# One kernel, two orders: the first transfers split over two queues, and another table of planned times

## The chip, the core and the metric

The kernel runs on one core of a Trainium2 chip. The metric is device time in microseconds (us) for one execution; less is better. The core has engines that run side by side, each through its own list of instructions in the order in which they were written: TensorE (PE, matrix products and transposes; its weight loads are shown as PEld), VectorE (DVE), ScalarE (ACT), GpSimd (POOL) and SyncE (SP, which here only starts transfers). Engines wait for one another through semaphores. Transfers (DMA) are started by an instruction on SP or ACT and then run by themselves on 16 shared DMA engines.

## The reference

Two layers, each a gated convolution (A) and a feed-forward network (B), with a residual around each. S is 2048 rows, D is 512, F is 1792; everything is bf16.

```
def A(q, k, v, shift_k, ssm_k, ssm_D):
    k_shift = sum over t in 0..3 of shift(k, t) * shift_k[:, t]   # short causal filter per channel
    kv = k_shift * v
    y  = causal convolution of kv with ssm_k along S               # 2048 taps, by FFT
    return q * (y + kv * ssm_D)

def B(x, w_gate, w_up, w_down):
    return (silu(x @ w_gate) * (x @ w_up)) @ w_down

x = A_q
for layer in (0, 1):
    x = x + A(layernorm(x), A_k, A_v, A_shift_k, A_ssm_k, A_ssm_D)
    x = x + B(layernorm(x), B_w_gate, B_w_up, B_w_down)
```

The factor that the layer norm feeds (`q` in A) is only multiplied in at the end, so the convolution of kv with ssm_k is the same in both layers and is computed once.

## The kernel before

**Blocks.** The 2048 rows are cut into four blocks c = 0..3 of 512 rows, and each block into two halves h of 256 rows. A triple (layer, c, h) names a unit of the feed-forward network, so there are 16 units. The convolution works by blocks: a block of ssm_k (`hn`, transposed to `hs`) and a block of kv become spectra `H` and `X` by matrix products with a table of cosines and sines (`fwd`), spectra are multiplied (`product`) into `Z`, and a product with the transposed table (`inv`) gives `Y`.

**Opening.** Nothing but this is on the way to the first feed-forward unit: load the first ssm_k block (`load_h`, line 412), the first k block (`load_k`, line 417) and the four filter taps per channel (`load_taps`, line 1033); transpose each on PE (lines 540, 431 and 1086); build diagonal matrices `dg` from the taps (lines 1091, 1093, 1097); apply the short filter on PE (`shift_mul`, line 560, shown as line 387, the helper `mm`) and multiply by v on DVE (line 575); spectra, products, inverse; then `n` and `xc` (lines 886 to 891), the statistics (line 796), `rstd` on POOL (line 801), `z` (line 851), its transposes on PE (`ptz`, line 903), copied to `zT` on ACT and DVE (lines 908, 906). Then unit (0,0,0) starts.

**Feed-forward unit.** `ffn`: 14 column blocks of F in groups of 4, 4, 4 and 2. PE writes gate and up products into PSUM (`pf`, four buffers), ACT takes them out as `sg` (line 949) and `ht` (line 953), DVE multiplies them (line 956), PE multiplies with `wd_sb` into `pd` (line 969). While these run, the other engines do the convolution and the layer norms of later blocks (`conv`, `prologue`).

**What sets the order.** The kernel records every step as an `Op` with an engine and an assumed cost, and `Plan.forward` lays out each engine's list: among the steps that can go next it takes the one with the earliest possible start, and among equals the one with the smallest due time. The due times are the table `DUE`, one entry for each op in the order of recording (`plan.dues(DUE)`, line 1188). The chip then runs each engine's list as it stands. Assumed delays from the issue of a transfer to its landing are constants such as `LH0` (first ssm_k block) and `LK0` (first k block). They shape the order and nothing else.

**Fillers.** Where the layout leaves PE idle for over 0.5 us in its first 32 us, `issue` puts in matrix products of the identity with itself whose result nobody reads (`wm`, line 1193); there are 24 at the start and 6 later. They wait for `ident`, which POOL makes (masks.py, lines 197 and 199).

**Choices by unit.** Small tables say which engine does a step for a given (layer, c, h): `ST1` and `ST2` put the statistics of a layer norm on ACT in place of DVE, `N_ACT` and `Z_ACT` put the normalising step on ACT, and `X_PE` adds the residual on PE with a product by the identity (line 928) in place of DVE. For (0,0,0) and (0,0,1) the first prologue has its own path, so the entries of `ST2`, `Z_ACT` and `N_ACT` for these two are not read; the last unit (1,3,1) adds its residual on PE whether or not `X_PE` has it.

**The first issues.** `HQ` chooses the order:

```
    if HQ == "ACT":
        tr = load_taps()
        k0 = load_k(0, -69.8, after=[tr])
    elif HQ == "k":
        ...
    else:
        h0 = load_h(0, "SP", -70)
        k0 = load_k(0, -69.9, after=[h0])
        tr = load_taps([k0])
```

With `HQ == "ACT"` the load `h0` has already been put on ACT's own queue (line 1029). After these, SP issues the row for ssm_D (`drow`, line 1046), the first v block (`vt`), the first x block (`xc`), the second ssm_k and v blocks, the gate weights, and two transposing transfers of the table (`inv`, line 1104).

Of the kernel before, what the change touches and what calls it, by code (L numbers as in the profile page):

```python
# [13 lines left out]
ACT = mybir.ActivationFunctionType  # L14
# [7 lines left out]
ST2 = lambda l, c, h: (l, c, h) in {(0, 0, 0), (0, 2, 1), (1, 2, 1)}  # L22
# [4 lines left out]
Z_ACT = lambda l, c, h: (l, c, h) in {(0, 0, 1), (0, 2, 0), (1, 0, 0), (1, 1, 0), (1, 1, 1)}  # L27
N_ACT = lambda l, c, h: (l, c, h) in {(0, 0, 1), (0, 2, 1), (0, 3, 0), (1, 0, 0), (1, 1, 1), (1, 3, 1)}
GROUPS = (4, 4, 4, 2)
TINY = 0.2  # L30
LH0 = 3.3
LK0 = 4.2
HQ = 'h'
# [4 lines left out]
X_PE = lambda l, c, h: (l, c, h) in {(0, 0, 0), (0, 2, 1), (1, 1, 0), (1, 3, 1)}  # L38
RINGS = {}
DUE = [2, 0, 0, 6, 3, 7, 5, 0, 6, 12, 18, 24, 32, 10, 12, 14, 8, 18, 24, 26, 28, 22, 24, 31, 37, 35, 44, 40, 46, 53, 38, 58, 41, 46, 43, 49, 46, 51,  # L40
       64, 80, 69, 96, 76, 88, 80, 90, 50, 56, 57, 71, 78, 85, 66, 65, 72, 68, 60, 62, 70, 1, 54, 59, 56, 77, 58, 74, 61, 84, 104, 60, 148, 204, 211,
       217, 84, 87, 91, 94, 102, 96, 99, 101, 108, 114, 73, 113, 115, 118, 126, 89, 103, 106, 111, 120, 104, 112, 119, 121, 131, 139, 143, 170, 193,
       176, 200, 132, 108, 122, 135, 145, 126, 139, 150, 130, 141, 143, 155, 148, 160, 153, 165, 173, 179, 158, 162, 172, 166, 175, 183, 171, 179,
       188, 184, 188, 195, 192, 196, 207, 201, 205, 212, 153, 159, 169, 166, 185, 191, 212, 203, 197, 206, 231, 215, 219, 225, 234, 238, 209, 217,
       214, 226, 229, 235, 231, 240, 233, 250, 238, 245, 250, 255, 261, 269, 293, 298, 295, 303, 241, 253, 252, 254, 309, 325, 263, 265, 311, 313,
       247, 259, 256, 258, 267, 269, 327, 329, 315, 317, 274, 338, 323, 265, 265, 272, 283, 287, 277, 298, 292, 299, 301, 304, 314, 320, 327, 317,
       322, 328, 332, 343, 350, 352, 369, 391, 395, 412, 414, 424, 417, 433, 440, 448, 462, 454, 461, 464, 467, 483, 486, 496, 493, 508, 345, 334,
       375, 369, 363, 356, 382, 393, 271, 284, 302, 297, 313, 324, 240, 260, 305, 283, 308, 320, 391, 398, 474, 481, 452, 464, 388, 402, 441, 450,
       419, 431, 421, 436, 471, 477, 500, 489, 526, 561, 543, 578, 224, 326, 331, 353, 404, 422, 511, 532, 549, 567, 585, 603, 645, 663, 680, 691,
       706, 719, 761, 750, 787, 854, 793, 781, 821, 829, 869, 883, 882, 893, 817, 824, 843, 872, 887, 905, 930, 942, 281, 307, 336, 364, 345, 360,  # L50
       353, 381, 362, 376, 416, 463, 443, 371, 386, 380, 393, 393, 407, 402, 440, 465, 493, 502, 410, 445, 423, 455, 432, 460, 454, 469, 477, 519,
       511, 476, 500, 484, 505, 523, 528, 532, 535, 541, 537, 558, 545, 577, 554, 572, 563, 582, 597, 616, 651, 572, 586, 581, 614, 589, 609, 598,
       624, 656, 668, 694, 607, 619, 624, 636, 633, 645, 642, 654, 674, 685, 703, 659, 679, 677, 688, 703, 711, 716, 719, 724, 731, 548, 550, 562,
       570, 574, 591, 593, 595, 602, 614, 621, 628, 640, 634, 642, 644, 647, 662, 665, 674, 672, 687, 738, 773, 744, 774, 781, 783, 799, 803, 807,
       814, 826, 838, 832, 840, 842, 845, 860, 865, 863, 878, 720, 732, 729, 741, 738, 749, 746, 758, 775, 825, 834, 755, 767, 764, 776, 773, 785,
       782, 793, 820, 873, 895, 790, 802, 799, 811, 808, 820, 843, 859, 866, 886, 904, 851, 871, 860, 876, 884, 916, 912, 924, 919, 991, 1028, 999,
       834, 843, 849, 852, 864, 881, 885, 899, 902, 916, 924, 954, 978, 960, 978, 981, 983, 997, 1003, 1000, 1016, 966, 988, 972, 981, 990, 995,
       1012, 1015, 1019, 1027, 1034, 1048, 1040, 1047, 1055, 1058, 1115, 1120, 1118, 1133, 887, 909, 898, 904, 942, 930, 955, 917, 1050, 1058, 1028,
       1036, 973, 986, 1017, 1025, 995, 1003, 1039, 1047, 976, 981, 1006, 1014, 1065, 1076, 1094, 1088, 1100, 1106, 1122, 1144, 1069, 1102, 1108,
       1075, 1089, 1115, 1095, 1082, 1165, 1183, 1177, 1200, 1122, 1206, 1128, 1149, 1133, 1209, 1221, 1250, 1237, 1262, 1275, 1302, 1340, 1325,  # L60
       1330, 1344, 1357, 1322, 1335, 1347, 1352, 1388, 1396, 1366, 1374, 1390, 1401, 1368, 1379, 1408, 1419, 1431, 1438, 1444, 1450, 1316, 967, 1215,
       1395, 1156, 1167, 1184, 1197, 1239, 1262, 1277, 1289, 1462, 1473, 1488, 1500, 1512, 1523, 1540, 1568, 1586, 1635, 1659, 1647, 1677, 1683,
       1680, 1688, 1702, 1716, 1659, 1670, 1693, 1701, 1665, 1692, 1710, 1729, 1747, 1777, 1804, 1815, 1834, 1864, 1852, 1878, 1896, 1913, 921, 933,
       930, 941, 938, 950, 947, 959, 982, 1061, 1070, 956, 968, 965, 976, 978, 991, 987, 998, 1006, 1087, 1078, 997, 1009, 1008, 1020, 1019, 1031,
       1030, 1042, 1049, 1096, 1104, 1041, 1053, 1052, 1064, 1112, 1222, 1192, 1237, 1213, 1250, 1291, 1287, 1113, 1140, 1122, 1135, 1130, 1144,
       1139, 1156, 1178, 1227, 1253, 1148, 1161, 1157, 1172, 1166, 1223, 1174, 1190, 1233, 1270, 1262, 1183, 1195, 1196, 1232, 1205, 1218, 1214,
       1227, 1256, 1279, 1288, 1235, 1247, 1244, 1256, 1273, 1301, 1296, 1308, 1304, 1316, 1305, 1317, 1314, 1325, 1327, 1340, 1336, 1347, 1355,
       1428, 1462, 1349, 1362, 1357, 1369, 1371, 1384, 1379, 1391, 1399, 1454, 1471, 1392, 1406, 1401, 1413, 1410, 1422, 1419, 1431, 1456, 1480,
       1488, 1436, 1454, 1445, 1459, 1484, 1501, 1497, 1509, 1504, 1534, 1323, 1337, 1329, 1336, 1339, 1342, 1364, 1361, 1368, 1376, 1383, 1395,
       1389, 1396, 1398, 1401, 1437, 1440, 1449, 1447, 1462, 1552, 1564, 1558, 1565, 1567, 1570, 1585, 1588, 1595, 1605, 1612, 1619, 1631, 1625,  # L70
       1632, 1634, 1637, 1653, 1656, 1666, 1663, 1678, 1532, 1534, 1506, 1517, 1514, 1526, 1523, 1535, 1536, 1548, 1579, 1624, 1606, 1545, 1557,
       1554, 1566, 1563, 1574, 1571, 1583, 1597, 1650, 1672, 1580, 1607, 1589, 1602, 1598, 1612, 1615, 1642, 1653, 1663, 1685, 1633, 1680, 1641,
       1675, 1689, 1706, 1698, 1742, 1705, 1749, 1713, 1617, 1625, 1632, 1635, 1646, 1654, 1659, 1703, 1707, 1723, 1741, 1758, 1770, 1764, 1800,
       1803, 1806, 1826, 1830, 1840, 1842, 1852, 1771, 1802, 1788, 1801, 1827, 1830, 1845, 1849, 1856, 1890, 1907, 1918, 1929, 1950, 1953, 1964,
       1976, 1981, 2006, 2011, 2009, 2024, 1726, 1710, 1721, 1747, 1780, 1792, 1767, 1755, 1857, 1873, 1905, 1913, 1888, 1893, 1890, 1898, 1859,
       1868, 1803, 1809, 1792, 1800, 1790, 1795, 1924, 1936, 1947, 1953, 1959, 1965, 1988, 1977, 2057, 1978, 2039, 1985, 2084, 2064, 2070, 2006,
       2097, 2077, 2022, 2090, 2051, 2108, 2134, 2146, 2097, 2119, 2156, 2169, 2181, 2206, 2194, 2240, 2259, 2267, 2275, 2265, 2270, 2331, 2338,
       2311, 2317, 2289, 2295, 2287, 2300, 2333, 2343, 2309, 2321, 2351, 2363, 2374, 2380, 2386, 2392, 2090, 2012, 2024, 2041, 2063, 2074, 2085,
       2108, 2216, 2404, 2415, 2433, 2451, 2465, 2477, 2489, 2502, 2526, 2514, 2538, 2556, 2550, 2544, 2553, 2561, 2566, 2574, 2628, 2635, 2615,
       2622, 1711, 1732, 1719, 1737, 1728, 1752, 1737, 1757, 1794, 1831, 1870, 1746, 1762, 1755, 1767, 1763, 1775, 1772, 1784, 1828, 1840, 1879,  # L80
       1781, 1804, 1794, 1814, 1805, 1819, 1814, 1825, 1846, 1862, 1969, 1822, 1837, 1849, 1863, 1875, 1901, 2039, 1908, 2046, 2053, 2065, 2061,
       1892, 1904, 1907, 1924, 1916, 1935, 1925, 1940, 1971, 2030, 2060, 1933, 1945, 1942, 1960, 1951, 1972, 1960, 1992, 2000, 2043, 2069, 1977,
       1996, 1986, 2001, 1995, 2013, 2004, 2017, 2035, 2051, 2077, 2012, 2029, 2021, 2034, 2059, 2090, 2086, 2125, 2103, 2132, 2139, 2193, 2095,
# [240 lines left out]
def kernel(  # L324
# [707 lines left out]
    def load_taps(after=()):  # L1032
        return add("SP", 0.5, lambda: nc.sync.dma_start(out=tapR.t[:], in_=A_shift_k.rearrange("(dt p) j -> dt p j", p=P)), w=[tapR],
                   lat=3.3, due=-70, after=after)
    if HQ == "ACT":
        tr = load_taps()
# [150 lines left out]

    plan.dues(DUE)

# [37 lines left out]
```

## Time and profile before

| | |
|---|---|
| median of 4 runs | 348.02 us (347.11 to 348.46) |
| the profiled execution's own time | 348.21 us |
| its span, first to last instruction | 346.4 us |
| PE | busy 340.0 us, 98% of the span, 2617 matrix products in the records |
| DVE, ACT, POOL | busy 279.4, 257.6 and 42.4 us |
| DMA | 22.96 MB, the busiest stretch is the first 10% of the span |

The span is cut from the first to the last instruction of the program; the time of an execution also holds what lies around it, here 1.81 us. "Busy" for PE is not PE at its peak, since matrix products are pipelined and their ends are modelled. In the chain of waits the steps are followed back from the last instruction; an engine that is idle off that chain costs nothing.

### The profile page before, as it was taken

What the parts mean: (1) busy time and instruction counts of PE and PEld (TensorE: products, weight loads), DVE (VectorE), ACT (ScalarE), POOL (GpSimd) and SP (SyncE); (2) the same over time, 40 slices, a digit from 0 to 9 for tenths busy, and PEclk for the clock granted to TensorE, in tenths of its full rate; (3) what the DMA queues carried; (4) which work ended last, traced back from release to release, by engine and by line L of the source; (5) the groups of instructions that cost most, each with busy time, mean ns of one, the idle gap of its engine ahead of it and who ended that gap; (6) DMA issues with size and microseconds to landing.
All of it is one profiled execution on the core that took longest, in us unless ns stands there. A gap on an engine that the chain in (4) does not pass through costs nothing.

```text
span 346.4 us, 6603 instructions
## 1 busy us (share of the span) xinstructions
PE 340.0 (98%) x2617; PEld 249.2 (72%) x2617; DVE 279.4 (81%) x472; ACT 257.6 (74%) x503; POOL 42.4 (12%) x46
## 2 busy tenths in 40 slices
PE   7999999999999999999999999999999999999996
PEld 6655867777686867768586867768676867777684
DVE  6898999999999998999999999959998425535111
ACT  5998997857989957838988999569684645556452
POOL 2200011103321001101201010301301000000000
PEclk9999999999999999999999999999999999999999
DMA  7999401010251173200132012210101200100101
GB/s 267 338 318 332 112 7 25 0 32 0 51 134 33 30 110 106 77 16 2 46 66 44 2 44 79 61 32 1 32 30 34 61 2 0 32 0 17 45 2 31
DMA packets 42089, 22.96 MB, mean 66 GB/s; under 512 B 33861, under 2 KB 39882, under 8 KB 42058
## 3 DMA queue, kind: packets, MB, share of 16 engines
q1 hardware_dynamic: 41914, 22.48, 25.1%
q8 instruction: 20, 0.33, 0.4%
q14 instruction: 11, 0.09, 0.1%
q10 hardware_dynamic: 144, 0.07, 0.1%
HBM read 12.33 MB, written 2.10 MB: 42 GB/s over the span
## 4 chain that ended last, share of the span: by engine, by line
PE 86%; ACT 8%; POOL 1%; DVE 1%; DMA 1%; issue 1%; POOLq 0%
PE pf L387 51%; PE pd L969 26%; PE ps L387 6%; PE ps L521 1%; DMA hs<-hr 1%; ACT ht L953 1%; ACT sg L949 1%; POOL rstd L827 1%; PE wm L1193 1%; ACT jk L821 1%; ACT jk L815 1%; ACT H L482 1%; ACT X L482 1%; ACT hr L642 1%; PE pt L540 1%
## 5 line engine op out<-in xcount | busy, mean ns | idle before, releaser
L387 PE MATMUL pf<-zT,wg_sb 128*128 128x256 bf16 x896 | 116.1, 273 | 0.3 <-ACT sg L949 0.2
L387 PE MATMUL pf<-zT,wu_sb 128*128 128x256 bf16 x896 | 116.1, 273 | 0.1
L969 PE MATMUL pd<-wd_sb,ht 128*128 128x512 bf16 (+1 forms) x462 | 104.2, 373 | 0.0
L387 PEld LDWEIGHTS <-wg_sb 128*128 128x128 bf16 x896 | 87.6, 98 | 18.7 <-issue 0.9
L387 PEld LDWEIGHTS <-wu_sb 128*128 128x128 bf16 x896 | 87.6, 98 | 14.3 <-issue 0.3
L949 ACT ACTIVATE sg<-pf 128x512 bf16<-128x512 f32 x112 | 67.1, 604 | 18.7 <-PE pf L387 18.7
L953 ACT CAST ht<-pf 128x512 bf16<-128x512 f32 x112 | 65.6, 589 | 20.7 <-PE pf L387 19.8
L969 PEld LDWEIGHTS <-ht 128*128 128x128 bf16 x462 | 45.2, 98 | 44.7 <-DVE ht L956 0.2
L956 DVE TENSOR_TENSOR ht<-ht,sg 128x1024 bf16<-128x1024 bf16 x64 | 39.5, 619 | 29.9 <-ACT ht L953 29.8
L801 POOL TENSOR_TENSOR rstd<-ve,nhalf 128x2 f32<-128x2 f32 x24 | 26.5, 1106 | 217.3 <-DVE ve L799 197.4
L796 DVE BATCH_NORM_STATS2 bnst<-xc 128x6 f32<-128x512 bf16 x48 | 31.0, 685 | 3.9 <-ACT xc L995 3.3
L1005 ACT CAST dn<-pd 128x512 bf16<-128x512 f32 x24 | 13.4, 589 | 24.6 <-PE pd L969 20.4
L704 DVE TENSOR_TENSOR t<-X,G 128x2048 bf16<-128x2048 bf16 x18 | 22.0, 1220 | 0.0
L708 DVE TENSOR_TENSOR t<-X,G 128x2048 bf16<-128x2048 bf16 x18 | 22.0, 1220 | 0.0
L482 ACT ACTIVATE X<-ps 128x512 bf16<-128x512 f32 x32 | 17.8, 604 | 2.2 <-PE ps L387 2.2
L1008 DVE TENSOR_TENSOR xc<-xc,dn 128x1024 bf16<-128x1024 bf16 x12 | 8.3, 689 | 12.6 <-ACT dn L1005 12.5
L827 POOL TENSOR_TENSOR rstd<-ve,nhalf 128x2 f32<-128x2 f32 x8 | 11.7, 1459 | 51.7 <-ACT ve L825 51.7
L482 ACT ACTIVATE H<-ps 128x512 bf16<-128x512 f32 x24 | 13.6, 615 | 3.4 <-PE ps L387 3.4
L718 DVE TENSOR_TENSOR Z<-Z,t 128x2048 bf16<-128x2048 bf16 x12 | 14.7, 1222 | 0.2
L716 DVE TENSOR_TENSOR t<-t,t 128x2048 bf16<-128x2048 bf16 x12 | 14.6, 1221 | 0.0
L387 PE MATMUL ps<-hs,fwd 128*128 128x512 bf16 x40 | 12.1, 379 | 0.6 <-ACT hs L544 0.4
L873 DVE TENSOR_TENSOR n<-n,Yk 128x1024 bf16<-128x1024 bf16 x15 | 10.4, 690 | 2.4 <-ACT n L846 1.6
(108 smaller groups left out, 324.0 us busy)
## 6 DMA issues: line engine op xcount, KB each, us to landing
hn<-in_A_ssm_k_dram SPq DMA_DIRECT2D x4, 512.0 KB, 5.4
vt<-in_A_v_dram SPq DMA_DIRECT2D x4, 512.0 KB, 5.3
xc<-in_A_q_dram SPq DMA_DIRECT2D x4, 512.0 KB, 6.2
out_dram<-xc SPq DMA_DIRECT2D x15, 128.0 KB, 1.8
wg_sb<-in_B_w_gate_dram SPq DMA_DIRECT2D x1, 1792.0 KB, 12.8
wu_sb<-in_B_w_up_dram SPq DMA_DIRECT2D x1, 1792.0 KB, 7.4
wd_sb<-in_B_w_down_dram SPq DMA_DIRECT2D x1, 1280.0 KB, 12.7
kn<-in_A_k_dram SPq DMA_DIRECT2D x1, 512.0 KB, 5.2
```

What stands on the lines that cost most here:

```text
L387: nc.tensor.matmul(o, lhsT=lhsT, rhs=rhs, start=(n == 0), stop=(n == len(terms) - 1))
L482: add("ACT", act(D), lambda: nc.scalar.activation(out=view(), in_=ps.t[:], func=ACT.Copy, scale=scale), r=[ps], w=[(buf, keys)], conv=conv)
L704: dve(n * D, lambda t1=t1, part=part: nc.vector.tensor_mul(out=t1.t[:], in0=x.t[:, sl, 0, :], in1=g.t[:, sl, part, :]), [(x, key(slots, (0 ...
L708: dve(n * D, lambda t2=t2, part=part: nc.vector.tensor_mul(out=t2.t[:], in0=x.t[:, sl, 1, :], in1=g.t[:, sl, 1 - part, :]), [(x, key(slots ...
L718: dve(n * D, lambda t1=t1, part=part: nc.vector.tensor_add(out=z.t[:, sl, part, :], in0=z.t[:, sl, part, :], in1=t1.t[:]), [t1], [zk], con ...
L796: add("DVE", 0.6, lambda st=st, i=i: nc.vector.bn_stats(out=st.t[:], in_=xs[c].t[:, i, :]), r=[(xs[c], (i,))], w=[st])
L801: add("POOL", pw, lambda: nc.gpsimd.tensor_tensor(out=rstd.t[:], in0=ve.t[:], in1=nhalf.t[:].to_broadcast((P, n)), op=ALU.pow), r=[ve, nha ...
L827: add("POOL", PW, lambda: nc.gpsimd.tensor_tensor(out=rstd.t[:], in0=ve.t[:], in1=nhalf.t[:].to_broadcast((P, n)), op=ALU.pow), r=[ve, nha ...
L949: add("ACT", act(D), lambda ps=ps, o=o, sg=sg: nc.scalar.activation(out=sg.t[:, o:o + 2, :], in_=ps.t[:], func=ACT.Silu), r=[ps], w=[(sg, ...
L953: add("ACT", act(D), lambda ps=ps, o=o, ht=ht: nc.scalar.copy(out=ht.t[:, o:o + 2, :], in_=ps.t[:]), r=[ps], w=[(ht, (o // 2,))], due=(uni ...
L956: dve(n * W, lambda sg=sg, ht=ht: nc.vector.tensor_mul(out=ht.t[:], in0=ht.t[:], in1=sg.t[:]), [sg], [ht], due=(unit, k / pairs, 0.0, "h"))
L969: nc.tensor.matmul((pds[o] if not cs.start else pds[HP]).t[:, cs], lhsT=ht.t[:, q, o * P:(o + 1) * P], rhs=wt["d"].t[:, ft, cs], start=(ft ...
```

## The change

No function is changed. What differs is a handful of constants and the whole of `DUE`:

```
-ST2 = lambda l, c, h: (l, c, h) in {(0, 0, 0), (0, 2, 1), (1, 2, 1)}
+ST2 = lambda l, c, h: (l, c, h) in {(0, 2, 1), (0, 3, 1), (1, 2, 1)}
...
-Z_ACT = lambda l, c, h: (l, c, h) in {(0, 0, 1), (0, 2, 0), (1, 0, 0), (1, 1, 0), (1, 1, 1)}
-N_ACT = lambda l, c, h: (l, c, h) in {(0, 0, 1), (0, 2, 1), (0, 3, 0), (1, 0, 0), (1, 1, 1), (1, 3, 1)}
+Z_ACT = lambda l, c, h: (l, c, h) in {(0, 0, 0), (0, 0, 1), (0, 2, 0), (1, 0, 0), (1, 1, 0), (1, 1, 1)}
+N_ACT = lambda l, c, h: (l, c, h) in {(0, 0, 0), (0, 2, 1), (0, 3, 0), (1, 0, 1), (1, 1, 1)}
...
-LH0 = 3.3
-LK0 = 4.2
-HQ = 'h'
+LH0 = 3.7
+LK0 = 4.5
+HQ = "ACT"
...
-X_PE = lambda l, c, h: (l, c, h) in {(0, 0, 0), (0, 2, 1), (1, 1, 0), (1, 3, 1)}
+X_PE = lambda l, c, h: (l, c, h) in {(0, 0, 0), (0, 0, 1), (0, 2, 1)}
...
-DUE = [2, 0, 0, 6, 3, 7, 5, 0, 6, 12, 18, 24, 32, 10, 12, 14, 8, 18, 24, 26, 28, 22, 24, 31, 37, 35, 44, 40, 46, 53, 38, 58, 41, 46, 43, 49, 46, 51,
...
+DUE = [2, 12, 0, 10, 8, 0, 6, 0, 0, 6, 12, 18, 25, 13, 19, 17, 15, 23, 29, 27, 33, 29, 31, 36, 42, 40, 49, 33, 40, 46, 42, 52, 45, 54, 47, 57, 50,
...
```

What this makes of the engines' lists: SP begins with the taps, then the first k block; the first ssm_k block is started by ACT, as ACT's first instruction, ahead of its table load. POOL makes `ident` first, and `eps`, the zeros of `kTb` and the ramps `fq` and `m4` after it. On PE the four tap transposes stand between the fillers and the transposes of `hn`, and there are 23 fillers in place of 24. DVE copies the taps out before the first copy of `hs`; ACT builds two `dg` blocks before its first copy of `hs`. On DVE the product at line 886 stands ahead of ACT's copy of the same PSUM tile (line 768) in place of behind it. Of the choices by unit, the ones that are read move these steps: the second statistics of (0,3,1) from DVE to ACT, a normalising step from (1,0,0) to (1,0,1) on ACT, that of (1,3,1) from ACT to DVE, and the residual on PE from (1,1,0) to (0,0,1). Apart from the one filler PE has the same matrix products in both programs. From 30 us on, every engine's list is a new interleaving of the same work.

## The prediction

> **What bounds the kernel now.** I read the page first: busy shares and the 40 slices.
>
> ```profile
> PE 340.0 (98%) x2617; PEld 249.2 (72%) x2617; DVE 279.4 (81%) x472; ACT 257.6 (74%) x503; POOL 42.4 (12%) x46
> PE   7999999999999999999999999999999999999996
> ```
>
> PE is busy from the first slice to the last, and both programs give it the same work, one filler apart. So the time can only move by what is not useful work on PE: the stretch before it starts, fillers, waits, the slow spacing at the start, and the 3.0 us from its end (343.4) to the end of the span. The waits of PE, longest first:
>
> ```profile
> PE wm L1193 <- POOL ident masks.py:199: 1.8, 1, 1.8
> PE ps L387 <- ACT hs L544: 0.4, 1, 0.4
> PE pd L928 <- DVE xc L891: 0.3, 1, 0.3
> PE pf L387 <- ACT sg L949: 0.2, 1, 0.2
> PE ps L387 <- DMA hs<-hr: 0.2, 1, 0.2
> ```
>
> These count from a modelled end; from start to start, less the normal spacing, PE loses 1.06 us in all after 35 us: 0.34 at 179.4 behind the transfer `hs`, 0.41 and 0.31 at 252 behind ACT. Everything else to be won or lost lies in the opening, so next the timeline from 0 to 13 us, SP, POOL and PE:
>
> ```profile
> 0.72 0.46 SPq L412 DMA_DIRECT2D hn<-in_A_ssm_k_dram  x1
> 1.24 0.49 SPq L417 DMA_DIRECT2D kn<-in_A_k_dram  x1
> 1.48 0.29 POOL masks.py:199 TENSOR_SCALAR_AFFINE_SELECT ident<-ident 128x128 bf16<-128x128 bf16 x1
> 1.78 0.36 SPq L1033 DMA_DIRECT2D tapR<-in_A_shift_k_dram  x1
> 1.83 2.74 PE L1193 MATMUL wm<-ident 128*128 128x128 bf16 x24 [1.83 <-POOL ident masks.py:199]
> 4.63 1.86 PE L540 MATMUL pt<-ident,hn 128*128 128x128 bf16 x16
> 6.52 0.29 PE L1086 MATMUL pt<-ident,tapR 4*128 4x4 bf16 x4
> 6.74 1.51 PE L431 MATMUL pt<-ident,kn 128*128 128x128 bf16 x16
> ```
>
> Fillers until 4.4, then `hn`, a wait of 0.28 for the taps, the taps, `kn`. Products of 128 columns start 0.107 us apart until 7.57 and 0.056 apart from then on, though the granted clock reads 1.00 throughout. From 8.09 to 22.0 PE has no wait, and the chain of waits goes through PE to 20.5. DVE is without a gap over 0.04 from 16.0, where it was released by what PE had just made, to 27.35. So a shift of PE at 8.09 goes through to the first unit at 34.7, and from there, PE being full, to the end.
>
> **Basis.** The sum starts from the profiled execution, 348.21 us (346.4 span, 1.81 around it), 0.19 above the median of 348.02, which I leave uncorrected: the four runs spread over 1.35. 0.3%, about what a measurement of this kernel can tell from no change, is 1.04 us, so slower begins at 349.06 and faster at 346.98.
>
> **Fillers sooner.** The two `ident` steps on POOL go from behind four others to the front: 1.21 to 1.77 becomes 0.72 to 1.29, and 23 fillers at 0.107 end at 3.80 in place of 4.4. Worth nothing alone, as PE then waits for data. The price is that `fq` and `m4` come 0.55 later, and with them the table: the second sine moves from 3.98 to about 4.5, its negation from 4.65 to 5.2. First needed at 8.09: hidden by 2.4 us; without that cover it would cost 0.55.
>
> **Taps.** Issued at 0.72 rather than 1.78. The first k leaves SP at about 1.14 rather than 1.24, `drow`, `vt`, `xc` and those behind about 0.5 sooner. When do the taps land? At most as late as now (released PE at 6.52, behind 1 MB); at least like the 64 KB stores at the end, 1.6 us. They are nearest to the latter, since nothing is ahead: by 3, before the fillers end. PE turns them at 3.80 to 4.02. That takes away the wait of 0.28 and the 0.22 of the four products: 0.50, if nothing else moves. DVE has the taps by 4.4, so `dg` is sooner; ACT's two `dg` (0.8) stand ahead of its copy of `hs`, but end by 6.0, before the first use of that copy.
>
> **The first ssm_k block.** ACT issues it at the same 0.72; its table load and first sine shift 0.46, within ACT's wait for DVE. But `kn` now sits on another queue. Now the two pass in line:
>
> ```profile
> DMA to landing us min/median/max: 3.6/3.6/3.6
> ```
> ```profile
> kn<-in_A_k_dram SPq DMA_DIRECT2D x1, 512.0 KB, 5.2
> out_dram<-xc SPq DMA_DIRECT2D x1, 64.0 KB, 1.6
> out_dram<-xc ACTq DMA_DIRECT2D x1, 64.0 KB, 1.7
> ```
>
> The first line is the answer for tile `hn` up to 3 us, the others are from the list of DMA issues. `hn` lands at 4.3 and PE turns it at 4.63. The only transfers on two queues at once are the last two lines, issued 0.16 us apart: neither waited for the other, which speaks for sharing. How long would sharing take? Bytes flow at 345 to 449 GB/s (windows of the trace):
>
> ```profile
> 2.25:3.25 1.00, 1.00 (x12) 1.00 (x11) 0.97 (x5) 0.51 (x1) 0.00 (x0) 1.00 1.01 345
> 3.75:5.00 1.25, 1.19 (x12) 1.03 (x11) 0.63 (x3) 0.63 (x1) 0.00 (x0) 1.00 1.19 390
> ```
>
> `hn` starts to move at 1.75, 1.03 after issue; `kn` would at 2.15. The remaining 510 KB of `hn` at half of 390 take 2.6, so its last byte passes at 4.8 rather than 3.7. Ends: 0 later (queues drained in order) and 1.1 later (equal shares). I take 1.1, by the two-queue rows. "DMA: Bandwidth & Descriptors" of the Trainium skill, section on issuing engines, speaks against this change: transfers started by different engines run on the same 16 DMA engines and interleave, and a second issuer saves only issue time. No row here shows that for two large loads.
>
> PE then has nothing from 4.02 to 5.73. At today's moment of the faster spacing, 7.57: 16 `hn` at 0.107 end at 7.44, one `kn` at 0.107 and 15 at 0.056 end at 8.39, where 8.09 is now: **+0.30**. With `hn` on time the same count gives 6.34, then 11.5 slow and 4.5 fast `kn`, end 7.82: -0.27.
>
> **The spacing.** Each us by which the change at 7.57 comes later, with PE at work, costs half a us. In this trace it came 5.74 after the first filler, with 0.54 idle between; with 1.71 idle it may come later. Ends: 0.49 sooner with the fillers (-0.25), or 5.74 after PE restarts, at 11.47, (11.47 - 7.57) / 2 = +1.95. No row decides, so I take about the middle, **+1.0**. "TensorE: Matmul & The Clock Gate" of the skill, Part 1, says that the array runs at half rate until it has been busy for a window of some 3.4 us, that runs freely; counted from 5.73 an estimate by it is 9.14, +0.8, and a total of 349.1. The trace's 5.74 is longer than one such window.
>
> **Row order at 28 us.** Now DVE waits 0.75 at line 886 behind ACT's copy of the same tile; in the new lists DVE goes first. But then ACT's row 0 waits for DVE and row 1 follows two ACT steps later, about 29.7, where it ends at 29.05 now, so line 889 gains 0.16 (29.89 to 29.73), and ACT's `zT` copy still comes behind two `ks` copies that wait for line 572. I take 0; at best -0.16.
>
> **After 35 us.** The spectra behind the wait at 179.4 are used 2.5 us of PE work later in the new list, while the last `hr` copy comes 1 us later on ACT: -0.34. At 252:
>
> ```profile
> 247.05 2.96 POOL L827 TENSOR_TENSOR rstd<-ve,nhalf 128x2 f32<-128x2 f32 x1 [4.30 <-ACT ve L825]
> 250.04 0.29 ACT L839 ACTIVATE nmr<-nm,rstd 128x1 f32<-128x1 f32 x1 [3.14 <-POOL rstd L827]
> ```
>
> ACT stands behind POOL with PE's buffers full. In the new list a second normalising step (0.81) also goes ahead of the next `sg`: +0.81 if POOL takes 2.96 again, -0.72 if it takes 1.46 like its neighbour at 241; mean +0.04. At three places PE gets back to a PSUM buffer after 1.09 us of other work (once now, without a wait): 0 to 0.3 together, +0.1. The statistics moved to ACT, 4.0 us, meet an ACT with 30 of 50 us busy from 250 to 300, and (1,3,1) takes 1.6 back: 0; without that room up to 2.4. Two residual products change units: 0. Together **-0.2**. The tail, from PE's end on, keeps its steps: 0.
>
> **Sum.** 0.30 + 1.0 - 0.2 = +1.1: 349.3. The taps' 0.50 is in it: it is why a delay of 1.1 costs only 0.30, together with `kn` moving under the fast spacing.
>
> **Rivals.**
> - *The first load keeps its pace* (faster, the other side): packets leave in order of issue, `hn` lands as now. Place: the gap between fillers and `hn`. Then -0.27, -0.25 (spacing sooner), -0.16, and of the 1.06 lost later some 0.7 gone: -1.4, 346.8; at best -1.7, 346.5. It decides if `hn` lands less than about 0.3 later. For it: `hn` has a head start of 0.4. Against it: the rows above.
> - *Shared, but the spacing turns on time* (no change): +0.30 - 0.2, 348.3; with `hn` half as late 348.1. Also where the change does not do what it says: if the taps were never on the path, their 0.50 vanishes into PE's idle stretch.
> - *New waits after 35 us*: POOL at 2.96 plus 0.81, and the three buffers at 0.3: +1.1 to the opening's +0.30, 349.6. Against it: between a product and its use at line 969 the new list has at least 2.18 us of PE work, now 1.73.
>
> **Chances.** Forecast 0.42, new waits 0.04: slower 0.46. On time 0.30: same. Pace kept 0.24: faster. The forecast's own range is 349.1 to 350.6. Over all, the low end leaves out the best part of the faster case: 346.7. The high end is +0.30, +1.95 and +0.2 for mid-run waits: 350.7.
>
> **What would show it.** Right: `hn` to landing 4.5 or more; an idle stretch of PE over 1 us between the taps and `hn`; the first `kn` products still 0.107 apart after 7.6; no wait at line 886 behind ACT; the wait behind `hs<-hr` gone. Wrong: `hn` landing by 4.6, PE's `hs` products starting before 8.0, or more than 1.5 us of PE waits after 35 us.

## The result, and the profile after

The changed kernel takes 348.54 us (median of 32 runs, 347.36 to 349.82), the kernel before 347.82 us (53 runs, 347.11 to 348.8): a ratio of 1.0023, 95% interval 1.0017 to 1.0029, or 0.7 us more. That is less than the 0.3% (1.04 us) that the prediction called about what a measurement can tell; with so many runs it is told, and it is small. The time lies in the range, 0.8 under the forecast, and under the 349.06 at which the prediction let "slower" begin. The profiled execution took 348.46 us with a span of 346.7, where before had 348.21 and 346.4.

The small difference is the sum of two large ones. From start to start of PE's products, PE reaches the first feed-forward product at 33.29 in place of 34.72, a gain of 1.43; after 35 us it loses 2.74 (0.44 at 205.7, 0.45 at 244.9, 1.85 at 251.5) in place of 1.06, a cost of 1.68. The opening, in two lines of the page's list of issues after (KB each, median us from issue to landing) and four of PE's timeline (start, busy time):

```profile
hn<-in_A_ssm_k_dram ACTq DMA_DIRECT2D x1, 512.0 KB, 3.5
kn<-in_A_k_dram SPq DMA_DIRECT2D x1, 512.0 KB, 4.5
```
```profile
1.34 2.64 PE L1193 MATMUL wm<-ident 128*128 128x128 bf16 x23 [1.34 <-POOL ident masks.py:199]
3.91 0.29 PE L1086 MATMUL pt<-ident,tapR 4*128 4x4 bf16 x4
4.29 1.85 PE L540 MATMUL pt<-ident,hn 128*128 128x128 bf16 x16
5.97 0.83 PE L431 MATMUL pt<-ident,kn 128*128 128x128 bf16 x12
```

The first ssm_k block lands 3.5 us after its issue, as before (3.6), and the k block 4.5 after, sooner than before (5.2). PE waits 0.2 for the block, turns its 16 pieces 0.107 apart, and the k block 0.056 apart from its first product: the closer spacing begins at 5.97, where before had 7.75 (its first closely spaced product; the prediction's 7.57 is the start of the last but one before it). Then PE's waits, from the list of waits after (us in total, times, longest):

```profile
PE pf L387 <- ACT sg L949: 1.7, 1, 1.7
...
PE pd L969 <- DVE ht L956: 0.6, 2, 0.3
PE ptz L903 <- DVE z L851: 0.6, 1, 0.6
PE ps L387 <- ACT hs L544: 0.4, 1, 0.4
```

The wait behind the transfer `hs<-hr` is gone, as predicted. New are two waits at 205.7 and 244.9 behind DVE's `ht`, and one of 1.7 at 251.5 behind ACT's `sg`. The timelines of POOL, DVE and ACT around it, after:

```profile
246.01 3.76 POOL L827 TENSOR_TENSOR rstd<-ve,nhalf 128x2 f32<-128x2 f32 x1 [3.04 <-ACT ve L825]
```
```profile
246.53 0.42 DVE L956 TENSOR_TENSOR ht<-ht,sg 128x512 bf16<-128x512 bf16 x1
...
248.00 1.22 DVE L708 TENSOR_TENSOR t<-X,G 128x2048 bf16<-128x2048 bf16 x1
249.25 1.23 DVE L716 TENSOR_TENSOR t<-t,t 128x2048 bf16<-128x2048 bf16 x1
```
```profile
249.80 0.30 ACT L839 ACTIVATE nmr<-nm,rstd 128x1 f32<-128x1 f32 x1 [3.93 <-POOL rstd L827]
...
252.13 0.81 ACT L846 ACTIVATE n<-xc,nmr,rstd 128x512 bf16<-128x512 bf16 x1
252.85 0.58 ACT L949 ACTIVATE sg<-pf 128x512 bf16<-128x512 f32 x1
```

POOL works 3.76 us on 128x2 numbers, a step that takes 0.69 elsewhere in this trace. ACT, whose next step needs POOL's result, stands still for 3.93. DVE runs its steps without a pause until 249.22, then pauses for 0.03 (line 716 needs the result of line 708), and POOL is done at 249.77, 0.55 after DVE stopped. In the kernel before, DVE stopped at 249.46 and POOL was done at 250.01, again 0.55 later; so too for the steps begun at 199.4 and 240.4 after. All eight of POOL's `rstd` steps over 2 us in the two traces end 0.54 to 0.55 after the start of DVE's first pause. So what looked like a duration is a wait for DVE. A pause is not the only way in, though, as the step at 241 in the kernel before shows:

```profile
240.98 1.22 DVE L704 TENSOR_TENSOR t<-X,G 128x2048 bf16<-128x2048 bf16 x1
241.29 1.46 POOL L827 TENSOR_TENSOR rstd<-ve,nhalf 128x2 f32<-128x2 f32 x1 [8.96 <-ACT ve L825]
242.11 1.22 DVE L708 TENSOR_TENSOR t<-X,G 128x2048 bf16<-128x2048 bf16 x1
```

Here POOL ended at 242.74, 0.55 after the first product (done at 242.20), though the second followed at once. In the trace after, POOL let the same change between the same two products go by, and took 2.56.

### The profile page after: what moved, and what is told of

It reads as the page before. It is cut to its first block, busy times and chain, and to the rows that moved or that the text cites. A ratio compares the mean times of both kernels' runs of the same rounds, so it can differ in the third digit from the quotient of the medians.

```text
span 346.7 us, 6601 instructions
## 1 busy us (share of the span) xinstructions
PE 339.0 (98%) x2616; PEld 248.4 (72%) x2616; DVE 278.3 (80%) x469; ACT 257.6 (74%) x509; POOL 44.6 (13%) x46
## 4 chain that ended last, share of the span: by engine, by line
PE 66%; DVE 18%; ACT 9%; POOL 3%; issue 1%; DMA 1%; DVEq 0%; ACTq 0%; POOLq 0%
PE pf L387 40%; PE pd L969 20%; PE ps L387 4%; DVE t L704 2%; POOL rstd L827 2%; DVE bnst L796 2%; DVE t L708 2%; DVE ht L956 2%; ACT sg L949 2%; ACT ht L953 1%; DVE t L716 1%; ACT X L482 1%; ACT jk L815 1%; ACT jk L821 1%; DMA hn<-in_A_ssm_k_dram 1%
## 5 line engine op out<-in xcount | busy, mean ns | idle before, releaser
L801 POOL TENSOR_TENSOR rstd<-ve,nhalf 128x2 f32<-128x2 f32 x23 | 24.0, 1045 | 203.2 <-DVE ve L799 203.2
L796 DVE BATCH_NORM_STATS2 bnst<-xc 128x6 f32<-128x512 bf16 x46 | 29.8, 685 | 2.2 <-ACT xc L995 1.7
L827 POOL TENSOR_TENSOR rstd<-ve,nhalf 128x2 f32<-128x2 f32 x9 | 16.9, 1873 | 65.0 <-ACT ve L825 65.0
L482 ACT ACTIVATE X<-ps 128x512 bf16<-128x512 f32 x32 | 18.7, 631 | 0.0
L821 ACT ACTIVATE jk<-xc,nm 128x512 bf16<-128x512 bf16 x18 | 13.0, 723 | 0.2
```

Of the source, the lines that this page charges most:

```text
L482: add("ACT", act(D), lambda: nc.scalar.activation(out=view(), in_=ps.t[:], func=ACT.Copy, scale=scale), r=[ps], w=[(buf, keys)], conv=conv)
L796: add("DVE", 0.6, lambda st=st, i=i: nc.vector.bn_stats(out=st.t[:], in_=xs[c].t[:, i, :]), r=[(xs[c], (i,))], w=[st])
L801: add("POOL", pw, lambda: nc.gpsimd.tensor_tensor(out=rstd.t[:], in0=ve.t[:], in1=nhalf.t[:].to_broadcast((P, n)), op=ALU.pow), r=[ve, nha ...
L827: add("POOL", PW, lambda: nc.gpsimd.tensor_tensor(out=rstd.t[:], in0=ve.t[:], in1=nhalf.t[:].to_broadcast((P, n)), op=ALU.pow), r=[ve, nha ...
```

## The experiments

Theory: the opening gained, and POOL's late `rstd` with ACT's order behind it lost more. Rivals: the opening's gain is a draw of the moment at which the spacing changes; the cost lies in ACT's order alone; the later waits have other causes. Edits are made on the finished order: `ahead(a, b)` puts op a ahead of op b in the lists, and leaves everything else as it was laid out. Times stand beside those of the kernel before on the same chip, whose medians were 348.05 (e1 to e4), 347.80 (e5 to e8), 347.65 (e9 to e11) and 347.70 (e12).

**The opening alone, in the lists of before (e1_opening).**

```
-        q = nc.sync if eng == "SP" else nc.scalar
+        q = nc.sync if eng == "SP" and b else nc.scalar   # first ssm_k block by ACT, at the head
+        ahead(5, 1)      # ident first on POOL
+        ahead(9, 8)      # taps ahead of the first k block
+        ahead(46, 30)    # tap transposes ahead of those of hn
...                       # two lines that set planned times, by which fillers are placed
```

> The kernel before, with the new opening alone: identity first on POOL, first ssm_k block issued by ACT, taps ahead of the first k block on SP, the four tap transposes ahead of those of the ssm_k block on PE. Every later list is that of before. Theory (the opening gained about 1.4 us, the new lists after 35 us lost about 1.7): PE is ready for the spectra about 1.2 us sooner than before, the waits of PE after 35 us stay at about 1.1, and the time is 346.6 (0.9 to 1.5 under before). Rival 1 (the gain was a draw of the moment at which the product spacing changes, not an effect of the order): 347.5 to 348, with the spacing changing at a moment that has no fixed distance to the first filler. Rival 2 (whatever PE gains early is given back at the waits behind POOL): as before, 347.8, with waits of over 2 us after 35 us.

347.91 us, ratio 1.0003 (0.9989 to 1.0017): nothing that can be told from no change. PE is at the first unit at 33.51, but from the list of waits of this run:

```profile
PE ps L387 <- DMA hs<-hr: 1.0, 1, 1.0
```

This wait, 0.2 in before, stood at 178 us. The theory's 346.6 is out. The time does not separate the rivals, since 347.91 is in the range of rival 1 and is "as before" for rival 2, and the profile speaks for both: the closer spacing begins 4.15 after the first filler where before had 5.92, and what PE wins early it partly loses at 178, another wait than rival 2 named.

**The block on ACT's queue alone (e2_split).** The first line of the diff above and no other.

> The kernel before, with one edit: the first ssm_k block is issued by ACT in place of SP, so that SP begins with the first k block; the taps stay behind the k block. Theory (two loads on two queues do not slow the first): the ssm_k block lands 3.5 to 3.6 us after its issue, the k block by 5.3, the taps by about 6, the wait of 0.28 for the taps goes: 0.2 to 0.4 us under before, 347.5. Rival (equal shares, as the prediction took it): the ssm_k block lands 4.5 us or more after its issue, PE idles 0.8 longer ahead of its transposes, time 348.3 to 349.

350.32 us, ratio 1.0064 (1.0044 to 1.0084). The list of issues of this run:

```profile
hn<-in_A_ssm_k_dram ACTq DMA_DIRECT2D x1, 512.0 KB, 5.1
kn<-in_A_k_dram SPq DMA_DIRECT2D x1, 512.0 KB, 3.5
```

Both were issued at 0.72, and neither theory holds: the k block passed first at full pace, and the ssm_k block behind it. By 3.5 us 496 KB of the k block had begun to move and only 49 of the other's 512. It was no sharing but a line, and not the interleaving that the section "Issuing engines are not separate DMA queues" of "DMA: Bandwidth & Descriptors" in the Trainium skill states and the prediction cites. In the change the taps hold the k block back by 0.44, and the order turns round. Why the k block goes first when both are issued together is not shown. PE was idle for 1.57 ahead of the block.

**The identity first, alone (e3_ident).** Only `ahead(5, 1)`.

> The kernel before, with one edit: POOL makes the identity first, so that the fillers of PE begin about 0.5 us sooner. Loads are as before. Theory 1 (the spacing of products changes a fixed time after the first filler, 4.6 to 5.7): it changes about 0.5 sooner than before, worth 0.25 us: 347.6. Theory 2 (it changes at moments that have nothing to do with the program, at most some 3.4 us apart): no change of the median (347.8), and in the profile the change lies anywhere between 4.7 and 9 us.

347.87 us, ratio 1.0005 (0.9984 to 1.0026), runs from 346.93 to 350.51: too scattered to tell 0.25. In its profile the closer spacing begins with the second product after the idle stretch, at 4.85, at most 3.50 after the first filler; before had 5.92. A fixed distance (theory 1) is out.

**A pause for POOL (e4_gap).**

```
+        was = plan.ops[1246].emit           # DVE ht<-ht,sg at 246.5
+        def with_gap():
+            was()
+            nc.vector.memset(gap[:], 0.0)
+            nc.vector.tensor_scalar(out=gap[:], in0=gap[:], scalar1=1.0, scalar2=None, op0=ALU.mult)
+        plan.ops[1246].emit = with_gap
```

> The changed kernel, with one edit: behind the DVE product ht<-ht,sg at 246.5 us DVE runs two tiny steps on a 128x1 tile, the second of which depends on the first, so that DVE pauses for a moment while POOL has its rstd step in hand. Theory (POOL's step ends about half a us after the first pause of DVE, whatever its own work of 0.69, and PE's wait of 1.85 at 251.5 stands behind it): rstd at 246 takes 1.2 to 1.6 in place of 3.76, the wait of PE at 251.5 shrinks to under 0.3, time 1.4 to 1.8 us under the changed kernel, 346.9. Rival 1 (a pause of DVE does not matter, POOL's step is long by itself in this place): rstd stays over 2.5 and the time within 0.3 of the changed kernel. Rival 2 (the second normalising step ahead of the next sg on ACT is the cost): the wait shrinks by no more than 0.8.

346.72 us, ratio 0.9975 (0.9957 to 0.9993): by the medians 1.8 under the changed kernel, by the ratios 1.7. DVE and POOL in its timeline:

```profile
246.76 0.06 DVE L1208 MEMSET gap<- 128x1 f32 x1
246.87 0.15 DVE L1209 TENSOR_SCALAR gap<-gap 128x1 f32<-128x1 f32 x1
```
```profile
246.55 0.81 POOL L827 TENSOR_TENSOR rstd<-ve,nhalf 128x2 f32<-128x2 f32 x1 [4.18 <-ACT ve L825]
```

Two tiny steps with a pause of 0.05 between them are enough: POOL takes 0.81 in place of 3.76, even less than the 1.2 to 1.6 of the theory, and PE has no wait at 251. The theory holds, rivals 1 and 2 fall. A pause of 0.03 between two long products was enough elsewhere; here no run separates the pause from the kind of the two steps.

**The order on ACT alone (e5_sg_first).** The changed kernel with `ahead(1299, 1263)`: the next `sg` ahead of the second normalising step.

> The changed kernel, with one edit: on ACT, in the pile at 250 us, the next sg goes ahead of the second normalising step, as it does in the kernel before. The rstd step on POOL is left as it is. The prediction priced this order at 0.81. Theory A (ACT is released by POOL, and what stands between that and the next sg delays PE one for one): the wait of PE at 251.5 shrinks from 1.85 to about 1.0, time 0.8 under the changed kernel, 347.7. Theory B (POOL's long step is the whole cost, and PE's buffers are empty too early for the order to matter): less than 0.3.

347.69 us, ratio 0.9995 (0.9977 to 1.0013), 0.85 under the changed kernel; POOL still takes 3.07. The wait, from the list of waits:

```profile
PE pf L387 <- ACT sg L949: 0.6, 1, 0.6
```

From start to start PE loses 0.79 here and 0.31 at 253, so 1.10 in place of 1.85. Theory A: up to 0.75 of the 1.85 came from the order, near the 0.81 at which the prediction priced it. POOL was also done 0.2 sooner against PE's list in this execution, which the run does not separate.

**The pause in the kernel before (e6_before_gap).** The edit of e4_gap at op 1247 of the kernel before.

> The kernel before, with one edit: two tiny dependent steps on DVE behind its ht<-ht,sg at 246.8 us, just after POOL's rstd step is released at 247.05. Theory (POOL gets its turn in the next pause of DVE, whichever lists surround it): rstd takes 0.8 in place of 2.96, PE's waits of 0.41 and 0.31 at 252 go, and the time falls by 0.7 to 347.2. Rival (the pause helped in the changed kernel for another reason, such as a later transfer): rstd stays near 2.96, time as before.

346.90 us, ratio 0.9971 (0.9957 to 0.9984). POOL takes 0.69 in place of 2.96, and no wait of PE is left at 252. The rival falls. The opening of this run is that of before, instruction for instruction, and its timeline reads:

```profile
4.63 1.37 PE L540 MATMUL pt<-ident,hn 128*128 128x128 bf16 x16
...
6.16 1.07 PE L431 MATMUL pt<-ident,kn 128*128 128x128 bf16 x16
```

Here the 16 pieces take 1.37 where before had 1.86, the spacing closes at 5.33 in place of 7.75, and PE is at the first unit at 33.69 in place of 34.72. One kernel's opening thus differs by 1.03 between two executions.

**More work ahead of the block (e7_cover).** e4_gap with `warm("pf", 0, 4)` behind the tap transposes.

> The changed kernel with the pause of e4_gap, and four more fillers of PE between the tap transposes and those of the first ssm_k block, 0.43 us, so that PE is not idle while that block is on its way. Theory (the moment of the faster spacing needs a stretch of 3.4 us with PE busy, which an idle stretch before the block lands can spoil, and a spoilt one costs up to 1.7 us): the upper group of the times of e4_gap, 3 of 12 above 348.4, is gone, all within 1.7 of the lowest, and the median falls by 0.1 to 0.4 to about 346.4. Rival (idle stretches of this size do not matter): the scatter stays, and the median rises by up to 0.2, as the block is turned later.

346.66 us, ratio 0.9963 (0.9948 to 0.9979), 345.86 to 347.89. The upper group is gone, but the spread is 2.0 and the median has not moved: not decided.

**Three pauses (e8_gaps).** The edit of e4_gap at ops 1246, 1100 (`ht` at 199.7) and 1014 (between the products at 241).

> The changed kernel with the pause of e4_gap and two more of the same kind: behind the DVE step ht<-ht,sg at 199.7, and between the two products t<-X,G at 241. Theory (all long rstd steps of POOL are waits for a pause of DVE, and the late products ht at 205.7 and 244.9, 0.45 each of PE's wait, stand behind them): the rstd step at 199.4 falls from 3.23 to about 1, that at 240.4 from 2.57 to about 1.5, both waits of PE shrink to under 0.1 of excess, time 0.5 to 0.9 under e4_gap, 346.0. Rival (these two waits of PE have another cause, DVE's long steps ahead of ht): rstd falls and the time stays within 0.3 of e4_gap.

346.05 us (345.30 to 346.72, 6 runs), ratio 0.9939 (0.9915 to 0.9963): the fastest median here, 1.75 under before on the same chip and 2.5 under the changed kernel by the medians, 2.9 by the ratios. POOL takes 0.95 at 200.4, and both waits behind `ht` are gone. The step at 241 took 1.42. In e4_gap, e5_sg_first and e7_cover, without a pause there, it took 1.42 or 1.43 too, and no wait stood at 244.9. So the third pause did nothing, and the 2.56 of the changed kernel's profile belongs to that execution and not to its lists. In the same way POOL's step at 167 took 3.43 in e4_gap, with 0.36 lost by PE at 189, and 0.76 in the changed kernel's own profile, with no edit ahead of it.

**The block in line behind the taps (e9_inline).** e8_gaps with `q = nc.sync` for every ssm_k load and `ahead(8, 7)`.

> The kernel e8_gaps (the changed kernel with the three pauses of DVE), with one edit: the first ssm_k block is issued by SP, right behind the taps, with the first k block behind it, in place of by ACT at the same time as the taps. Theory A (what counts is which load's first packet comes first, not the number of queues): the ssm_k block is issued 0.44 later and lands at 4.7 to 4.9 in place of 4.2 to 4.5, the k block about where it was in the kernel before, and the time is 0.2 to 0.5 over e8_gaps, 346.4. Theory B (the second queue itself is the gain of the opening): the opening goes back to that of the kernel before, the time rises by 0.6 or more, 346.7 or over.

348.17 us, ratio 1.0003 (0.9985 to 1.0020): by the time theory B. PE's timeline shows the wait:

```profile
5.20 1.90 PE L540 MATMUL pt<-ident,hn 128*128 128x128 bf16 x16 [0.99 <-DMA hn<-in_A_ssm_k_dram]
```

The block was issued at 1.16 and landed 4.0 later, at 5.16, where it landed at 4.4 in e8_gaps (3.7 after its issue). With the closer spacing from 7.95 (about 7.7 in e8_gaps, worth 0.1) PE is at the first unit at 34.73 in place of 34.22, so some 0.4 later, as theory A has it. The 4.0 is not the mark of a queue: on ACT's queue the block took 3.5 to 4.0 in the profiles where it went first. The runs lost 2.1, and the profiled one, 347.14, was the fastest of 12. In the same way 5 of the 6 runs of e2_split took at least 350.1 where the profiled one took 348.56. In both, PE is idle for more than a microsecond ahead of the block. An idle stretch may push the closer spacing later still in most runs; no profile caught such a run, so this is argued and not shown.

**Pauses and more fillers (e10_gaps_cover).** e8_gaps with the line of e7_cover.

> The kernel e8_gaps with four more fillers of PE between the tap transposes and those of the first ssm_k block. The candidate for the fastest. Theory (a shorter idle stretch ahead of the block spoils fewer stretches of work that the faster spacing needs): no time above 347.2, median as e8_gaps or up to 0.2 under, 345.9. Rival (the moment of the faster spacing is free within 3.4 us whatever the fillers do, and the four fillers only turn the block later): 346.0 to 346.3, the scatter as in e8_gaps.

346.21 us (345.77 to 346.71, 5 runs), ratio 0.9955 (0.9942 to 0.9968). Not faster than e8_gaps: the rival.

**Opening and pause in the lists of before (e11_open_gap).** The diffs of e1_opening and e6_before_gap together.

> The kernel before, with the new opening (as in e1_opening) and the pause of DVE at 247 us (as in e6_before_gap). Theory (at one and the same moment of the faster spacing the new opening has PE at the first unit 0.6 us sooner, and fillers that begin 0.5 sooner bring that moment 0.5 sooner, worth 0.2 more, but the wait for the transposing transfers at 178 us gives a part of it back): 0.2 to 0.6 under e6_before_gap, 346.5, with a wait of 0.6 to 1.2 at 178. Rival 1 (nothing takes the gain back): 346.1 or less. Rival 2 (the new opening is worth nothing, the difference of the two profiles was the draw of the moment alone): as e6_before_gap, 346.9.

346.81 us, ratio 0.9986 (0.9973 to 0.9999), against 346.90 for e6_before_gap: by the time rival 2. By the trace PE is at the first unit at 33.61 with the closer spacing from 5.72, where the two openings of before (34.72 with 7.75, 33.69 with 5.33) would have 33.86 at that moment: 0.25 gained. At 178 us it waits 0.51 longer than a product's spacing. Both effects are smaller than the times of this comparison can tell.

**No fillers (e12_no_fillers).** e8_gaps without the 23 fillers.

> The kernel e8_gaps with the 23 fillers at the start left out, so that PE's first product is that of the taps. Theory (products come closer together 3.4 to 6.8 us after PE begins to work, at a moment that no list sets within that stretch): the change falls between 7.4 and 11.2 in place of 4.8 to 8.1, with the block at 4.5 that costs half of about 3 us, time 347.4 to 347.7. Rival (the moment is free of PE's work, or the idle stretch ahead of the block matters more than the fillers): within 0.3 of e8_gaps, 346.1. It also shows when the taps land: by 3.0 in the prediction.

347.56 us, ratio 0.9993 (0.9981 to 1.0005), 1.5 over e8_gaps by the medians. PE's timeline:

```profile
2.56 0.29 PE L1086 MATMUL pt<-ident,tapR 4*128 4x4 bf16 x4 [2.56 <-DMA tapR<-in_A_shift_k_dram]
4.78 1.90 PE L540 MATMUL pt<-ident,hn 128*128 128x128 bf16 x16 [1.93 <-DMA hn<-in_A_ssm_k_dram]
```

The taps are there at 2.56. The close spacing starts at 9.74, 4.96 after the first piece of the block and 7.18 after the taps. The theory holds: fillers that nobody reads are worth about 1.5 us here.

## Why the prediction was right or wrong

**Right in sign and within the range, by luck.** The forecast was +1.1, measured is +0.7. By the prediction's own limits that is "same", to which it gave 0.30, against 0.46 for slower. Two of its rivals came true together and nearly cancelled: the pace that the first load kept, and POOL with new waits after 35 us. The sum had +1.3 in the opening and -0.2 after 35 us, the profiles have -1.4 and +1.7. Its own list of what would prove it wrong was met three times: `hn` landed by 4.6, products on `hs` began at 6.64, and PE lost 2.74 after 35 us.

**Fillers and taps.** Starts and ends came within 0.1 of what was worked out (first filler at 1.34, taps turned from 3.91), and the taps landed by 3 (2.56 in e12_no_fillers). That the earlier start is worth nothing alone fits e3_ident, whose time cannot be told from before. What the fillers are worth as such, e12_no_fillers shows: without them the closer spacing began at 9.74.

**The first block (+0.30).** Wrong: the step that failed is equal shares. It was read from two stores of 64 KB and did not carry over to two loads of 512 KB. Of the two ends that the prediction kept, "queues drained in order" was the right one: the landing came at 4.2 in place of 5.4. e2_split shows what the step lacked: one load waits for the other, and without the lead of 0.44 that the taps give it, the ssm_k block is the one that waits.

**The spacing (+1.0).** Wrong, and the step that cost most. It took the 5.74 of one trace for a property of the order. In 13 profiles with fillers the close spacing begins between about 3.5 and 6.6 after the first filler, with the same instructions at 3.50 (e6_before_gap) and at 5.92 (before). The section Part 1 of "TensorE: Matmul & The Clock Gate" in the Trainium skill says that the window of about 3.4 us runs freely, and that one window has to be busy; a change one to two windows after the first work is what that gives, and these 13 profiles agree with that. Each microsecond of that moment is worth 1.03 / 2.42 = 0.43 at the first unit. So of the 1.43 between the two profiles (7.75 - 5.97) x 0.43 = 0.76 comes with that moment, which is mostly a draw of the execution. At one and the same moment the changed kernel gains 0.55 (33.14 in e4_gap against 33.69 in e6_before_gap, with the spacing closing at 5.35 and 5.33), of which the first issues alone give 0.25 (e11_open_gap); the rest lies between 8 and 34 us in the other lists. The fillers' earlier start of 0.49 should add 0.49 x 0.43 = 0.2 on average, an estimate that no run here resolves.

**Row order (0).** The wait at line 886 is gone, and a new one of 0.6 behind `z` ends at 31.87. The rows were not separated.

**After 35 us (-0.2).** The -0.34 at `hs<-hr` was right. The step that failed is POOL at 252: 2.96 "again" or 1.46 "like its neighbour", mean +0.04. It took 3.76, and with ACT's order, whose price of 0.81 was about right, PE lost 1.85 in place of 0.72. The duration is not a property of POOL's step but of what DVE runs beside it. In the section "Who interferes with whom" of "SBUF — State Buffer", the Trainium skill says that DVE and GpSimd share one pair of ports under an exclusive lock. That POOL's step falls from 3.76 to 0.81 (e4_gap) and from 2.96 to 0.69 (e6_before_gap) by two tiny steps in DVE's list agrees with that. When POOL gets its turn is only partly shown: at DVE's first pause at the latest, in the steps over 2 us, and often already between two steps without a pause, as at 241.29 before. In all six profiles with no edit at this place (before, after, e1_opening, e2_split, e3_ident, e5_sg_first) the step took 2.95 to 3.76 and ended 0.55 after the start of the pause behind line 708, so "again" was the better of the two values; the one trace that the prediction had could not tell this. The two waits behind `ht` were not foreseen at all: the pause at 199.7 took the first away, and the second belonged to the one execution.

## What to carry to other kernels

When an engine's small step has scattered durations, look for what ends it before taking a mean: here each one over 2 us ended 0.5 us after another engine's first pause, and two tiny steps at the right place in that engine's list gave back more than the whole change moved. Two profiles are two draws: compare an opening at the same moment of the changing product spacing, or take a second profile of the same kernel, before a difference of a microsecond is put down to an edit. A gain at the start reaches the end only if no list further on waits for something that did not move with it.

## What the runs showed of the hardware

- POOL's `rstd` on 128x2 takes 0.69 alone and up to 3.76 beside DVE steps of 0.42 to 1.22 that follow one another without a pause; two dependent steps on 128x1 let it in (0.69 to 0.99). At the same place in the same lists it can take 1.42 in one execution and 2.56 in another.
- Two loads of 512 KB on two queues, issued together, went one behind the other: landing 3.5 and 5.1 after issue. With a lead of 0.44 for the second it went first (3.5), and the other landed 4.5 after issue.
- With fillers, the product spacing halves between 3.5 and 6.6 us after PE's first work, at a moment that differs between executions of one opening, while the profile's row of the granted clock reads full throughout.
